# Two exchanges in a hand-written order: P V of unit 13 and the first row of o and wo in the seventh stretch, half of wo and a turn of o in the fifth

## The chip, the cores and the metric

The kernel runs on one core of a Trainium2 chip. The metric is the device time of one execution in microseconds (us), median over runs. Traces and profiles are of one profiled execution each.

## The reference, cut to what matters

The input x has 2048 tokens of width 640. It is layer-normed to xn, and two things are computed from it: attention over the last 512 cached keys with 32 heads of width 192, and a gate from two selected tokens that pass a small feed-forward block. The result is x + s * g.

```
def _A_ref(x, k_cache, v_cache, wq, wo):          # x is xn here
    q = (x @ wq).reshape(B, Sq, Hq, Dh)           # 32 heads of 192
    k = k_cache[:, :, Sk - W:, :]                 # W = 512 keys
    v = v_cache[:, :, Sk - W:, :]
    scores = einsum("bhqd,bhkd->bhqk", q, k) * (Dh ** -0.5)
    p = softmax(scores)
    o = einsum("bhqk,bhkd->bhqd", p, v)
    return o.reshape(B, Sq, Hq * Dh) @ wo         # s

return x + s * silu(_B_ref(xn, ...))
```

## The kernel before, in words

The attention is cut into units. A unit n is a pair of heads and a block of 128 tokens; there are 256. Units come in steps of four (512 tokens of one pair of heads), and steps in the order: groups of four heads, then blocks of 512 tokens, then the two pairs of heads of the group. So units 0 to 3 are the first 512 tokens for the first pair of heads, units 4 to 7 the same tokens for the second pair, units 8 to 15 the next 512 tokens for both pairs, and so on.

For a unit TensorE computes the scores of both heads (`scores`, lines 331 and 338: a part of depth 128 and one of depth 64), VectorE their negated row maximum (`row_max`, line 346), ScalarE the exponentials with their sums (`exps`, line 353), and a DMA transpose on SyncE's queue turns the probabilities from `pexp` into `pT` (`p_turn`, line 358). Then TensorE multiplies them with v (`o_mul`, line 372: 8 matmuls of 192 columns into one PSUM tile `o_ps`; this is "P V" below), VectorE or ScalarE scales the product with the reciprocal sums into `o_sb` (`o_out`, lines 387 and 385), and a second DMA transpose turns `o_sb` into `oT` (`o_turn`, line 393).

The last product joins both pairs of heads of a group: a row w of o and wo (`w_mul`, line 420) takes the turned o of one unit of each pair, three chunks of 128 of each, and multiplies them with the group's wo. It does this for two halves of 320 output columns, six matmuls each, so a row has twelve, into two PSUM tiles `w_ps`; in each half the first three matmuls use the first pair's unit, the last three the second pair's. Row 0 uses units 0 and 4, row 1 units 1 and 5, row 2 units 2 and 6. `w_out` (lines 432 and 434) puts a half into `s_acc`. The weights wo of a group come in two loads of 480 KB (`wo_load`, line 140): `wo.g.0` has the three chunks of the first pair, `wo.g.1` those of the second. So the first three matmuls of a half need the first load and the last three the second.

Units are worked in stretches. The first two hold two units each, every later one three: stretch 4 (counted from 0) has units 10 to 12, stretch 6 has units 16 to 18. While the scores and exponentials of a stretch are worked, the products P V, the projections q and the rows w of earlier stretches are put between them. There is no scheduler: the schedule is manual, and each engine and each DMA queue works in the order in which the program emits its instructions. Of the stretches 0 to 10 this order is written out by hand, token by token, in the string `FIRST`; each begins with `S.j`, the scores of stretch j. From stretch 11 on the functions `stretch` and `end_stretch` write the order by a rule. The tokens that matter here are:

- `S.6`: scores of units 16 to 18; `M.n.h`, `E.n.h`: row maximum and exponentials of unit n, head h; `P.n`: turn of the probabilities
- `O.n` and `Oe.n.e`: P V of unit n and its scaling (e: `v` VectorE, `a` ScalarE); with `O.n.g` its PSUM tile comes from the pool `ps_p` and not from `ps_f`
- `T.j` and `T.j.lo.hi`: turn of o of stretch j, or of its units lo to hi alone. `T.2.0.1` turns unit 4, `T.2.1.3` units 5 and 6
- `W.w` and `We.w.e`: row w of o and wo, and its way into `s_acc`
- `wo.g.h`: the load of a half of wo

All DMAs named here, loads and transposes, are issued from SyncE, in program order. The PSUM pool `ps_p` has six buffers. Scores, the halves of a row and the `.g` tokens take their tiles from it, so the six score tiles of a stretch fill it, and later tiles get a buffer when its reader (an exp, a scaling, a copy) is done. The pool `ps_f` has two buffers, for the q projections and the other products P V.

Of the kernel before, what the change touches and what calls it, by code (L numbers as in the profile page):

```python
# [21 lines left out]
def kernel(ctx, tc, A_x, A_k_cache, A_v_cache, A_wq, A_wo, B_x, B_w_r, B_w_gate, B_w_up, B_w_down, out):  # L22
    nc = tc.nc
    P = 128
    _, S, D = A_x.shape
# [3 lines left out]
    W = min(4096, max(256, Sk // 4))  # L29
# [426 lines left out]
    M = {}  # L456
# [413 lines left out]
S.1 q.1.2 ap.5.g M.2.0 ap.7.g E.2.0 M.2.1 q.1.0.2.4 ap.6.g xT.4.6 q.1.0.0.2.g bn.10.0 qe.1.2.a M.3.0 M.3.1 R.0 bn.10.1 xT.6.8 E.2.1 qe.1.0.0.2.a qe.1.0.2.4.a q.1.1 P.2 bn.11.0 O.0 bn.11.1 bn.8.0 E.3.0 E.3.1 qe.1.1.a Oe.0.v P.1 bn.8.1   # L870
S.2 x.3.0.4 v.1 q.2.1.0.2 as.9 M.4.0 M.4.1 q.2.0 M.6.0 E.4.0 pw.8.12 E.4.1 q.2.2.g M.5.0 qe.2.1.0.2.a E.5.0 qe.2.0.v M.6.1 ap.10.g E.6.0 ap.9.g P.3 E.6.1 M.5.1 q.3.1 qe.2.2.v ap.8.v R.1 ap.11.g O.2 qe.3.1.v Oe.2.v E.5.1 
S.3 M.8.0 M.7.0 P.4 P.5 M.8.1 q.2.1.2.4 M.7.1 R.2 xT.8.10 M.9.0 as.13 bn.15.0 M.9.1 E.8.0 E.7.0 E.8.1 q.3.2 bn.14.0 xT.10.12 E.7.1 P.6 qe.2.1.2.4.a q.3.0.g qe.3.0.a qe.3.2.v E.9.0 E.9.1 O.1.g O.5.g O.4.g Oe.4.a Oe.1.v P.8 as.12 Oe.5.v O.3 
S.4 P.7 bn.15.1 M.10.0 q.4.1 M.11.0 M.12.0 M.11.1 Oe.3.a q.4.0 P.9 M.10.1 qe.4.1.v E.10.0 M.12.1 E.11.0 T.0 E.11.1 q.5.0.g E.10.1 wo.0.0 wo.0.1 T.2.0.1 E.12.0 E.12.1 R.3 qe.4.0.a O.8.g O.7 P.10 Oe.7.a qe.5.0.v T.1 Oe.8.v R.4 bn.14.1 pw.12.16 
S.5 ap.12.g O.6 M.13.0 P.11 E.13.0 M.15.1 Oe.6.a M.15.0 E.15.0 E.15.1 q.4.2 M.13.1 P.12 q.5.2.g M.14.1 M.14.0 qe.4.2.v O.9 E.13.1 Oe.9.a qe.5.2.v E.14.0 W.0 We.0.v E.14.1 
S.6 M.17.0 P.13 M.17.1 ap.14.g M.16.1 O.10 M.18.1 Oe.10.a M.16.0 ap.13.g E.17.0 q.5.1 E.17.1 qe.5.1.v T.2.1.3 E.16.0 R.5 O.12 O.11.g Oe.11.a M.18.0 E.18.0 Oe.12.a E.16.1 W.1 O.13.g We.1.v E.18.1 ap.15.g xT.13.16 xT.12.13 W.2 We.2.v P.15 Oe.13.a 
S.7 q.6.1 M.19.1 M.19.0 E.19.0 M.20.0 q.6.0 qe.6.0.v P.14 T.4 M.21.0 M.20.1 M.21.1 E.19.1 T.3 q.6.2.g k.2.1.a qe.6.1.a O.14 O.15.g R.6 E.20.0 q.7.1.g E.20.1 Oe.14.a P.17 qe.6.2.a E.21.0 Oe.15.v q.7.0 P.16 E.21.1 P.19 W.3 P.18 W.4 qe.7.1.v R.7 qe.7.0.v We.3.v O.19 We.4.a wq.2.a 
S.8 wq.3.a O.16 Oe.19.v M.22.0 v.2.a M.23.1 E.22.0 Oe.16.v k.3.0.a M.23.0 P.20 E.23.0 wo.1.0.a E.23.1 k.3.1.a T.5 M.22.1 M.24.0 P.21 q.7.2 E.24.0 O.17 Oe.17.v E.22.1 P.22 k.2.0.a W.5 qe.7.2.v M.24.1 We.5.a O.20 P.23 W.6 O.21 We.6.a E.24.1 Oe.20.a Oe.21.a O.18.g Oe.18.v P.24 
S.9 M.25.0 M.27.1 M.25.1 M.27.0 q.8.1 E.25.0 E.25.1 q.9.0 T.6 M.26.0 qe.8.1.v W.7 E.27.0 E.27.1 E.26.0 M.26.1 R.8 We.7.v P.25 qe.9.0.v E.26.1 q.8.0 T.7 
# [47 lines left out]
```

## Time and profile before

| | us |
|---|---|
| median of 3 runs | 790.81 |
| lowest and highest of them | 790.41, 791.25 |
| the profiled execution | 789.15 |
| its span | 787.4 |

The mean granted TensorE clock of the profiled execution is 0.999 of full speed. The span runs from the first to the last instruction of the trace; the execution's own time is 1.75 us longer. In the rows of the profile each line has a start or a sum in us, an engine, a line of the kernel, an operation, the tiles (out<-in), their sizes and a count. PE is TensorE's matmuls, PEld its weight loads, DVE VectorE, ACT ScalarE, POOL GpSimd, SPq the queue of SyncE, whose rows show how long an issue took, not the transfer. In the rows of DMA issues the last number is the time from issue to landing. A row that merges several instructions has their count behind it, and its length runs from the first start to the last end; as matmuls are pipelined, the time of a group is better taken from its start to the start of the next group.

### The profile page before, as it was taken

To read this page: it belongs to the slowest core of one execution; us is meant where nothing else is said; L and a number is where in the kernel's file an instruction comes from. 1 tells how busy PE (TensorE), PEld (TensorE's weight loads), DVE (VectorE), ACT (ScalarE), POOL (GpSimd) and SP (SyncE) were. 2 spreads that over 40 slices of the span, in tenths; PEclk is the share of its full clock that TensorE was granted. 3 is DMA by queue.
4 is the path that set the end of the run, shared out by engine and by line. 5 is a ranking of instruction groups with operands and counts; after the bars stand their busy time and mean duration, and the time that the engine had idled before them with its cause. 6 is when DMAs were issued, how large, how long until landed. Compare 5 with 4: busy or idle time off the path is not lost.

```text
span 787.4 us, 15694 instructions
## 1 busy us (share of the span) xinstructions
PE 781.8 (99%) x5767; PEld 482.8 (61%) x5767; DVE 621.7 (79%) x1238; ACT 479.4 (61%) x1299; POOL 179.5 (23%) x198
## 2 busy tenths in 40 slices
PE   8999999999999999999999999999999999999998
PEld 4566656666666666566666655666566666556666
DVE  7976678988888777777777777777788988777786
ACT  8975766565556655565665556565667865565652
POOL 3230000000010000000000699960000000165966
PEclk9999999999999999999999999999999999999999
DMA  9999998899889999999998899779997799997996
GB/s 262 214 202 229 204 199 132 164 175 202 166 147 219 184 195 217 142 221 198 191 222 144 181 180 188 158 141 174 202 172 138 143 193 184 183 194 152 177 167 148
DMA packets 453133, 143.80 MB, mean 183 GB/s; under 512 B 421358, under 2 KB 452720, under 8 KB 453056
## 3 DMA queue, kind: packets, MB, share of 16 engines
q1 hardware_dynamic: 447696, 138.04, 94.0%
q10 hardware_dynamic: 4672, 3.08, 1.4%
q0 software_dynamic: 688, 1.68, 0.9%
q8 instruction: 45, 0.74, 0.4%
q14 instruction: 32, 0.26, 0.1%
HBM read 39.98 MB, written 2.62 MB: 54 GB/s over the span
## 4 chain that ended last, share of the span: by engine, by line
PE 95%; DMA 2%; DVE 1%; ACT 1%; issue 0%; SPq 0%; POOL 0%; DVEq 0%
PE q_ps L317 26%; PE w_ps L420 26%; PE o_ps L372 21%; PE sc L331 14%; PE sc L338 8%; DMA oT<-o_sb 1%; DMA x_in<-in_A_x_dram 1%; ACT pexp L353 1%; DVE nm L346 0%; DVE stats L172 0%; POOL fin_o L447 0%; PE gu_ps L590 0%; ACT o_sb L385 0%; PE y_ps L627 0%; DVE fin_t L445 0%
## 5 line engine op out<-in xcount | busy, mean ns | idle before, releaser
L353 ACT ACTIVATE pexp<-sc,nm 128x512 bf16<-128x512 f32 x512 | 348.5, 697 | 264.1 <-issue 231.7
L346 DVE TENSOR_REDUCE nm<-sc 128x1 f32<-128x512 f32 x512 | 314.9, 682 | 70.9 <-PE sc L338 70.7
L317 PE MATMUL q_ps<-xnT,wq_p 128*128 128x512 bf16 (+1 forms) x985 | 225.4, 374 | 0.5 <-DMA wq_p<-in_A_wq_dram 0.5
L420 PE MATMUL w_ps<-wo_g,oT 128*128 128x320 bf16 (+1 forms) x1542 | 223.0, 298 | 0.1
L420 PEld LDWEIGHTS <-oT 128*128 128x128 bf16 x1542 | 150.4, 98 | 69.5 <-DMA oT<-o_sb 0.4
L372 PE MATMUL o_ps<-v_sb,pT 128*128 128x192 bf16 x2048 | 184.8, 246 | 0.0
L372 PEld LDWEIGHTS <-pT 128*128 128x128 bf16 x2048 | 171.4, 98 | 14.0 <-issue 2.8
L317 PEld LDWEIGHTS <-wq_p 128*128 128x128 bf16 x985 | 89.7, 98 | 122.8 <-issue 33.3
L387 DVE TENSOR_TENSOR o_sb<-o_ps,lsum 128x384 bf16<-128x384 f32 x240 | 132.0, 556 | 41.3 <-PE o_ps L372 22.7
L331 PE MATMUL sc<-kT,qT 128*128 128x512 bf16 x512 | 125.5, 379 | 0.1
L434 DVE TENSOR_TENSOR s_acc<-s_acc,w_ps 128x320 f32<-128x320 f32 x192 | 92.5, 483 | 30.7 <-PE w_ps L420 30.7
L353 ACT ACTIVATION_READ_ACCUMULATOR pexp<-sc,nm 128x1 f32 x512 | 110.2, 215 | 0.0
L309 ACT ACTIVATE qT<-q_ps 128x512 bf16<-128x512 f32 (+1 forms) x180 | 98.7, 604 | 0.0
L331 PEld LDWEIGHTS <-qT 128*128 128x128 bf16 x512 | 48.5, 98 | 42.0 <-issue 1.5
L338 PE MATMUL sc<-kT,qT 64*128 64x512 bf16 x512 | 70.2, 380 | 0.0
L338 PEld LDWEIGHTS <-qT 64*128 64x128 bf16 x512 | 18.0, 94 | 46.7 <-issue 35.8
L664 POOL TENSOR_TENSOR s_acc<-s_acc,xn 128x640 f32<-128x640 f32 x16 | 22.9, 1434 | 103.0 <-DVE s_acc L434 102.9
L643 POOL TENSOR_TENSOR xn<-xn,yh 128x640 bf16<-128x640 bf16 x32 | 44.6, 1394 | 2.7
L633 POOL DMA_DIRECT2D y_d<-y_sb x4 | 2.2, 544 | 181.2 <-DVE y_sb L630 181.2
L510 POOL DMA_DIRECT2D c_d<-cand x1 | 0.7, 725 | 162.8 <-DVE cand L508 162.8
L665 POOL TENSOR_TENSOR s_acc<-s_acc,x_fin 128x640 f32<-128x640 f32 x16 | 22.4, 1400 | 61.4 <-DVE s_acc L434 54.3
L642 POOL TENSOR_SCALAR yh<-y_bc,oh 128x640 bf16<-128x640 bf16 x32 | 25.6, 800 | 5.2 <-DMA y_bc<-y_d 3.6
(110 smaller groups left out, 234.1 us busy)
## 6 DMA issues: line engine op xcount, KB each, us to landing
wo_g<-in_A_wo_dram SPq DMA_DIRECT2D x15, 480.0 KB, 4.3
wq_p<-in_A_wq_dram SPq DMA_DIRECT2D x14, 480.0 KB, 4.6
v_sb<-in_A_v_cache_dram SPq DMA_DIRECT2D x15, 384.0 KB, 4.3
k_raw<-in_A_k_cache_dram SPq DMA_DIRECT2D x28, 192.0 KB, 3.2
pT<-pexp SPq DMA_TRANSPOSE x256, 3.6
x_fin<-in_A_x_dram SPq DMA_DIRECT2D x16, 160.0 KB, 2.7
wgu<-in_B_w_gate_dram SPq DMA_DIRECT2D x15, 128.0 KB, 3.3
wgu<-in_B_w_up_dram SPq DMA_DIRECT2D x15, 128.0 KB, 3.6
```

Of the source, the lines that this page charges most:

```text
L309: nc.scalar.activation(out=out, in_=in_, func=ACT.Copy, scale=scale)
L317: nc.tensor.matmul(q_ps, lhsT=wq_of[g * PAIRS + pr][:, dc, c * P:(c + 1) * P], rhs=xnT[:, t5 * 4 + lo:t5 * 4 + hi, dc, :], start=(dc == 0) ...
L331: nc.tensor.matmul(sc_of[n][hh], lhsT=qT_of[i][:, 2 * hh, u * P:(u + 1) * P], rhs=kp[:, :, 2 * hh, :], start=True, stop=False)
L338: nc.tensor.matmul(sc_of[n][hh], lhsT=qT_of[i][hs, 1, u * P:(u + 1) * P], rhs=kp[hs, :, 1, :], start=False, stop=True)
L346: nc.vector.tensor_reduce(out=nm_of[j][:, c:c + 1], in_=sc_of[n][hh], axis=AX.X, op=ALU.max, negate=True)
L353: nc.scalar.activation(out=pe_of[n][:, hh, :], in_=sc_of[n][hh], func=ACT.Exp, bias=nm_of[j][:, c:c + 1], scale=1.0, accum_out=l_of[j][:, ...
L372: nc.tensor.matmul(ps[:, hh, :], lhsT=pT_of[n][:, hh, jj, :], rhs=v_sb[:, hh, jj, :], start=(jj == 0), stop=(jj == NJ - 1))
L387: nc.vector.tensor_tensor(out=osb_of[j][:, m], in0=ps, in1=l_of[j][:, 2 * m:2 * m + 2].unsqueeze(2).to_broadcast([P, 2, Dh]), op=ALU.mult)
L420: nc.tensor.matmul(w_ps, lhsT=oT_of[j][:, stretches[j].index(n), c % 3, :], rhs=wo_of[g][:, c, lo:hi], start=(c == 0), stop=(c == CPG - 1))
L434: nc.vector.tensor_tensor(out=acc, in0=acc, in1=w_ps, op=ALU.add)
L642: nc.gpsimd.tensor_scalar(out=yh, in0=M["y_bc"][:, j, :], scalar1=M["oh"][:, n, j:j + 1], scalar2=0.0, op0=ALU.mult, op1=ALU.add)
L643: nc.gpsimd.tensor_tensor(out=xn[:, n, :], in0=xn[:, n, :], in1=yh, op=ALU.add)
```

## The change

Two pairs of tokens in the string `FIRST` change places. In stretch 4 (the fifth) the load of the second half of wo stands behind the turn of unit 4 and no longer ahead of it. In stretch 6 (the seventh) P V of unit 13 stands ahead of row 1 of o and wo and no longer behind it. Nothing else differs. The two lines, cut round the places:

```
-S.4 ... E.11.0 T.0 E.11.1 q.5.0.g E.10.1 wo.0.0 wo.0.1 T.2.0.1 E.12.0 E.12.1 R.3 qe.4.0.a O.8.g O.7 P.10 Oe.7.a ...
+S.4 ... E.11.0 T.0 E.11.1 q.5.0.g E.10.1 wo.0.0 T.2.0.1 wo.0.1 E.12.0 E.12.1 R.3 qe.4.0.a O.8.g O.7 P.10 Oe.7.a ...

-S.6 ... T.2.1.3 E.16.0 R.5 O.12 O.11.g Oe.11.a M.18.0 E.18.0 Oe.12.a E.16.1 W.1 O.13.g We.1.v E.18.1 ap.15.g xT.13.16 xT.12.13 W.2 We.2.v P.15 Oe.13.a
+S.6 ... T.2.1.3 E.16.0 R.5 O.12 O.11.g Oe.11.a M.18.0 E.18.0 Oe.12.a E.16.1 O.13.g W.1 We.1.v E.18.1 ap.15.g xT.13.16 xT.12.13 W.2 We.2.v P.15 Oe.13.a
```

Between the tokens `W.1` and `O.13.g` there is no instruction of another engine, so on the other engines nothing changes its order in stretch 6. In stretch 4 the same holds for SyncE's queue round the exchanged pair.

More of the change, by code (lines that the diff above doesn't have):

```diff
@@ L872 @@
 S.3 M.8.0 M.7.0 P.4 P.5 M.8.1 q.2.1.2.4 M.7.1 R.2 xT.8.10 M.9.0 as.13 bn.15.0 M.9.1 E.8.0 E.7.0 E.8.1 q.3.2 bn.14.0 xT.10.12 E.7.1 P.6 qe.2.1.2.4.a q.3.0.g qe.3.0.a qe.3.2.v E.9.0 E.9.1 O.1.g O.5.g O.4.g Oe.4.a Oe.1.v P.8 as.12 Oe.5.v O.3
-S.4 P.7 bn.15.1 M.10.0 q.4.1 M.11.0 M.12.0 M.11.1 Oe.3.a q.4.0 P.9 M.10.1 qe.4.1.v E.10.0 M.12.1 E.11.0 T.0 E.11.1 q.5.0.g E.10.1 wo.0.0 wo.0.1 T.2.0.1 E.12.0 E.12.1 R.3 qe.4.0.a O.8.g O.7 P.10 Oe.7.a qe.5.0.v T.1 Oe.8.v R.4 bn.14.1 pw.12.16
+S.4 P.7 bn.15.1 M.10.0 q.4.1 M.11.0 M.12.0 M.11.1 Oe.3.a q.4.0 P.9 M.10.1 qe.4.1.v E.10.0 M.12.1 E.11.0 T.0 E.11.1 q.5.0.g E.10.1 wo.0.0 T.2.0.1 wo.0.1 E.12.0 E.12.1 R.3 qe.4.0.a O.8.g O.7 P.10 Oe.7.a qe.5.0.v T.1 Oe.8.v R.4 bn.14.1 pw.12.16
 S.5 ap.12.g O.6 M.13.0 P.11 E.13.0 M.15.1 Oe.6.a M.15.0 E.15.0 E.15.1 q.4.2 M.13.1 P.12 q.5.2.g M.14.1 M.14.0 qe.4.2.v O.9 E.13.1 Oe.9.a qe.5.2.v E.14.0 W.0 We.0.v E.14.1
-S.6 M.17.0 P.13 M.17.1 ap.14.g M.16.1 O.10 M.18.1 Oe.10.a M.16.0 ap.13.g E.17.0 q.5.1 E.17.1 qe.5.1.v T.2.1.3 E.16.0 R.5 O.12 O.11.g Oe.11.a M.18.0 E.18.0 Oe.12.a E.16.1 W.1 O.13.g We.1.v E.18.1 ap.15.g xT.13.16 xT.12.13 W.2 We.2.v P.15 Oe.13.a
+S.6 M.17.0 P.13 M.17.1 ap.14.g M.16.1 O.10 M.18.1 Oe.10.a M.16.0 ap.13.g E.17.0 q.5.1 E.17.1 qe.5.1.v T.2.1.3 E.16.0 R.5 O.12 O.11.g Oe.11.a M.18.0 E.18.0 Oe.12.a E.16.1 O.13.g W.1 We.1.v E.18.1 ap.15.g xT.13.16 xT.12.13 W.2 We.2.v P.15 Oe.13.a
 S.7 q.6.1 M.19.1 M.19.0 E.19.0 M.20.0 q.6.0 qe.6.0.v P.14 T.4 M.21.0 M.20.1 M.21.1 E.19.1 T.3 q.6.2.g k.2.1.a qe.6.1.a O.14 O.15.g R.6 E.20.0 q.7.1.g E.20.1 Oe.14.a P.17 qe.6.2.a E.21.0 Oe.15.v q.7.0 P.16 E.21.1 P.19 W.3 P.18 W.4 qe.7.1.v R.7 qe.7.0.v We.3.v O.19 We.4.a wq.2.a
```

## The prediction

> **What bounds the kernel now.** I read the page first, then the chain of waits between 50 and 58.5 us, then the timelines of TensorE, its weight loads, ScalarE and SyncE's queue round the two places of the change, then the landing times of the DMAs issued there.
>
> ```profile
> span 787.4 us, 15694 instructions
> PE 781.8 (99%) x5767; PEld 482.8 (61%) x5767; DVE 621.7 (79%) x1238; ACT 479.4 (61%) x1299; POOL 179.5 (23%) x198
> PE 95%; DMA 2%; DVE 1%; ACT 1%; issue 0%; SPq 0%; POOL 0%; DVEq 0%
> 58.20:780.00 721.80, 721.80 (x5346) 447.90 (x5344) 569.03 (x1121) 428.68 (x1162) 156.57 (x145) 1.00 0.97 180
> ```
>
> The last row is the view by stretches of time: from 58.2 to 780 us TensorE is busy for all 721.80 us at the full granted clock. So whatever TensorE gains or loses before 58 us arrives at the end, unless a later wait on something other than TensorE takes it back. The question is only what TensorE does between 41 and 58 us, where both edits lie.
>
> ```profile
> 50.08 4.59 DMA oT<-o_sb
> 54.66 0.05 issue
> 54.71 1.40 PE w_ps L420 x9
> 56.11 0.66 PE o_ps L372 x8
> ...
> 52.76 1.48 PE L372 MATMUL o_ps<-v_sb,pT 128*128 128x192 bf16 x16
> 54.08 2.02 PE L420 MATMUL w_ps<-wo_g,oT 128*128 128x320 bf16 x12
> 55.94 0.82 PE L372 MATMUL o_ps<-v_sb,pT 128*128 128x192 bf16 x8
> 56.60 1.79 PE L420 MATMUL w_ps<-wo_g,oT 128*128 128x320 bf16 x12
> 58.23 1.46 PE L331 MATMUL sc<-kT,qT 128*128 128x512 bf16 x6
> ...
> 54.00 0.32 PEld L420 LDWEIGHTS <-oT 128*128 128x128 bf16 x3
> 54.70 1.07 PEld L420 LDWEIGHTS <-oT 128*128 128x128 bf16 x9 [0.39 <-DMA oT<-o_sb]
> ```
>
> The first four rows are the chain of waits. It goes through a DMA: the turn of o of units 5 and 6 (T.2.1.3), issued at 50.08, landed at 54.66, and TensorE went on at 54.71 with the nine matmuls that need it. The next five rows are TensorE in order: P V of units 12 and 11, row 1 (W.1), P V of unit 13, row 2 (W.2), the next scores. A row of twelve matmuls without a stall is W.2: 56.60 to 58.23, 1.63 us, 0.136 us each. W.1 takes from 54.08 to 55.94, 1.86 us. So it stalls for **0.23 us**, after its third matmul: unit 1's three chunks are loaded at 54.00, unit 5's not before 54.70. That is the only cost that the first edit can remove.
>
> **The change part by part: P V of unit 13 ahead of W.1.** It adds and removes no instruction. Unit 13's eight matmuls last 56.60 - 55.94 = 0.66 us, and they now run at 54.08, while the turn lands. They need their probabilities turned (P.13) and a free PSUM buffer.
>
> ```profile
> 48.70 1.28 SPq L358 DMA_TRANSPOSE pT<-pexp  x1
> pT<-pexp SPq DMA_TRANSPOSE x1, 3.3
> ...
> 53.74 0.22 ACT L353 ACTIVATION_READ_ACCUMULATOR pexp<-sc,nm 128x1 f32 x1
> 54.02 0.69 ACT L353 ACTIVATE pexp<-sc,nm 128x512 bf16<-128x512 f32 x1
> 54.60 0.19 ACT L353 ACTIVATION_READ_ACCUMULATOR pexp<-sc,nm 128x1 f32 x1
> 54.70 0.72 ACT L385 ACTIVATE o_sb<-o_ps,lsum 128x192 bf16<-128x192 f32 x2
> 55.91 0.19 ACT L353 ACTIVATION_READ_ACCUMULATOR pexp<-sc,nm 128x1 f32 x1
> ```
>
> P.13 is issued at 48.70 and lands 3.3 us later, at 52.0, well ahead of 54.08. The buffers are the finer point. The scores of units 16 to 18 hold all six buffers of the pool ps_p, and every later tile takes one that has been read out. By ScalarE's program order and the rows above, they come free so: the exp of 17.1 ends at 53.96, of 16.0 at 54.79, the two scalings of unit 11's o at 55.42, the exp of 18.0 at 56.10. The profile does not show which tile takes which buffer; I take them in the order of release. Then W.1's two halves now hold those of 17.1 and 16.0, and P V of 13 that of unit 11. After the change P V of 13 takes that of 17.1 (free at 53.96, so it starts at 54.08 as W.1 did), W.1's first half takes that of 16.0, its second half that of unit 11.
>
> So W.1, which could start at 54.08 + 0.66 = 54.74, waits for 54.79 plus the 0.05 us that the chain shows between a landing and TensorE's start: **54.84**. Its fourth matmul comes at 54.84 + 3 x 0.136 = 55.25, 0.6 us behind the landing of 54.66: the old stall is gone. Its second half starts at 55.66, behind 55.42: no wait. W.2 follows at 54.84 + 1.63 = 56.47 and finds buffers free since 56.10 (exp of 18.0) and about 56.4 (first eviction of W.1, wanted only at 57.3). It started at 56.60, so the gain is 56.60 - 56.47 = **0.13 us**. The bounds: 0.23 us if the first half gets an earlier buffer, and nothing if all of the gain waits elsewhere. I take 0.13, since its two ends are measured rows.
>
> No instruction changes its place on VectorE or ScalarE: the scaling of unit 13's o stays behind the exp of 18.1, over 1 us after its product is done either way. The queues of SyncE and GpSimd are not touched by this edit.
>
> What is late next is the chance of losing the 0.13 us again:
>
> ```profile
> 80.82 1.62 PE L331 MATMUL sc<-kT,qT 128*128 128x512 bf16 x6
> 81.02 0.56 DVE L387 TENSOR_TENSOR o_sb<-o_ps,lsum 128x384 bf16<-128x384 f32 x1 [2.97 <-PE o_ps L372]
> ```
>
> These six scores take 1.62 us against 1.46 at 58.23: a wait of 0.16 us on VectorE's scaling, which itself waits for TensorE's product of o. It moves with TensorE, so it gives nothing back. I found no other such gap up to 780 us, as the full row of 721.80 says.
>
> **The second half of wo behind the turn of unit 4.** Again nothing is added; SyncE's queue changes its order from T.0, wo.0.0, wo.0.1, T.2.0.1 to T.0, wo.0.0, T.2.0.1, wo.0.1.
>
> ```profile
> 40.41 0.57 SPq L140 DMA_DIRECT2D wo_g<-in_A_wo_dram  x1
> 41.03 0.48 SPq L140 DMA_DIRECT2D wo_g<-in_A_wo_dram  x1
> 41.61 1.18 SPq L393 DMA_TRANSPOSE oT<-o_sb  x1
> 42.90 1.33 SPq L358 DMA_TRANSPOSE pT<-pexp  x1
> ...
> wo_g<-in_A_wo_dram SPq DMA_DIRECT2D x1, 480.0 KB, 4.0
> wo_g<-in_A_wo_dram SPq DMA_DIRECT2D x1, 480.0 KB, 4.9
> oT<-o_sb SPq DMA_TRANSPOSE x1, 4.8
> ...
> 46.58 0.82 PE L372 MATMUL o_ps<-v_sb,pT 128*128 128x192 bf16 x8
> 47.24 1.79 PE L420 MATMUL w_ps<-wo_g,oT 128*128 128x320 bf16 x12
> 48.87 1.46 PE L331 MATMUL sc<-kT,qT 128*128 128x512 bf16 x6
> ```
>
> The issues follow each other at once, so the turn moves from 41.61 to 41.03 and the load from 41.03 to about 41.03 + 1.18 + 0.06 = 42.27; P.10 behind them stays at 42.90. Landings now: 44.4, 45.9 and 46.4 (issue plus the latency of its row), so they come in the order of the issues, with 1.5 us for the second half of wo and 0.5 us for the turn. Exchanged, the turn lands at about 44.9 and the load at about 46.4.
>
> Who needs them is row 0 (W.0) at 47.24: it takes 1.63 us to the next scores, the same as W.2, so it stalls for nothing now. The earlier turn therefore frees nobody. The later load is needed by its fourth matmul, at 47.24 + 0.41 = 47.65; at 46.4 it has 1.2 us to spare. By the full latency of 4.9 us from its new issue it would land at 47.2, still in time. I take **nothing** for this edit. Above is the rival below; below nothing is excluded, since TensorE waits for neither DMA here.
>
> The Trainium skill, page "DMA: Bandwidth & Descriptors", section "Rules for kernel authors", speaks against this edit: "Issue the DMA early, do compute, wait on its semaphore late". Here the time from issue to need falls from 47.65 - 41.03 = 6.6 us to 5.4 us; the trace's 4.9 us lies below both, so by the rule the edit is a loss of cover and by the rows not yet a loss of time.
>
> Sum: 787.4 - 0.13 = 787.3 us of span. The profiled execution took 789.15 us, 1.7 below the median of 790.81 that the three runs show (790.41 to 791.25); I carry the difference over: 790.81 - 0.13 = **790.7 us**.
>
> **Rivals.**
>
> *Wo late: slower.* If the second half of wo lands after 47.65, W.0's fourth matmul waits and everything behind it. It decides at a latency of 47.65 - 42.27 = 5.4 us.
>
> ```profile
> DMA to landing us min/median/max: 3.8/4.4/5.3
> wq_p<-in_A_wq_dram ACTq DMA_DIRECT2D x1, 480.0 KB, 6.2
> v_sb<-in_A_v_cache_dram ACTq DMA_DIRECT2D x1, 384.0 KB, 6.4
> ```
>
> Against it: none of the sixteen loads of wo took over 5.3 us (first row). For it: loads queued behind others near 71 us took 6.2 and 6.4. Then it lands at 48.7 and W.0 loses 1.0 us: 790.81 + 1.0 - 0.1 = 791.7 at most, 791.1 to 791.7 in general.
>
> *No stall to remove: a new wait instead of the old one.* T.2.1.3 landed 4.6 us after issue, where its neighbour P.13 took 3.3.
>
> ```profile
> 52.50:54.00 1.50, 1.50 (x17) 1.33 (x16) 1.50 (x4) 1.46 (x5) 0.00 (x0) 1.00 1.30 36
> q8 instruction: 1, 0.02, 2.5%
> ```
>
> From 52.5 to 54 the queues moved 36 GB/s, against 183 over the span, and one packet of instructions was fetched between 51.5 and 54.7. If that is an accident of the profiled execution, the turn usually lands at 50.08 + 3.3 = 53.4, W.1 does not stall now (it needs it at 54.49), and the change only adds the wait of 54.84 - 54.74 = 0.10 us: 790.9. For it: the hole in the traffic. Against it: instruction fetches follow the program, which is the same in every run.
>
> *A larger stall than the profile's.* If the turn commonly lands later still, P V of 13 covers up to its own 0.66 us: 790.81 - 0.66 = 790.15. Against it: 54.66 is already the late case beside its neighbours.
>
> *Full gain.* W.1's first half finds an earlier buffer: -0.23, 790.6.
>
> **How the numbers follow.** Chances: forecast 0.48, full gain 0.10, a new wait 0.20, wo late 0.13, larger stall 0.09. Likeliest is 790.7. The range takes in the spread of the three runs (0.40 below, 0.44 above their median) round the first three cases, which gives 790.2 to 791.35, and reaches to the other two: up to 791.7 for wo late, down to 789.9 for half of the larger stall with the spread. A measurement of this kernel can tell about 0.2%, 1.6 us, from no change: below 789.2 or above 792.4. No case reaches either bound by itself. Only the larger stall with its spread (789.75) and late wo with its spread (792.1) come near, so most of the chance is within: faster 0.04, same 0.90, slower 0.06.
>
> **What would show it.** In the profile after, the order at 54 us is P V, W.1, W.2 without P V between; W.1's twelve matmuls are near 1.63 us apart from start to next start, and no weight load of line 420 waits for the DMA of oT. A start of W.1 at 54.84 with the exp of line 353 just ahead shows the buffer's wait; at 54.74 it is the full gain. W.0 still takes 1.63 us; if it takes longer behind its third matmul, wo is late. The issues read wo_g, oT, wo_g, with wo landing before 47.65. The prediction is wrong if the scores at 58.23 move by other than 0.1 to 0.25 us, or if a TensorE gap appears after 58 us that was not there.

## The result, and the profile after

The changed kernel takes 792.41 us (median of 22 runs, 790.19 to 795.01) against 790.11 us before (22 runs, 789.21 to 791.47). The ratio is **1.0026, with a 95% interval of 1.0018 to 1.0034**: slower, where 0.1 us faster was forecast. The times spread twice as wide as before: ten lie from 790.2 to 792.0 and twelve from 792.3 to 795.0, with no wide gap between them. The twelve are called the upper group below. The profiled execution took 792.93 us and is one of them.

The page of the changed kernel, its span, busy times and shares of the chain of waits:

```profile
span 791.2 us, 15694 instructions
PE 782.4 (99%) x5767; PEld 482.7 (61%) x5767; DVE 621.8 (79%) x1238; ACT 480.1 (61%) x1299; POOL 179.7 (23%) x198
PE 91%; DMA 4%; ACT 2%; DVE 1%; issue 0%; SPq 0%; POOL 0%; ACTq 0%; DVEq 0%
```

The work is the same to 0.6 us of TensorE, but the chain now spends 4% in DMAs where it spent 2%. Which DMAs, the chain between 43 and 84 us tells (start, length, what):

```profile
43.28 0.57 SPq L140
...
43.96 5.92 DMA pT<-pexp
...
49.99 1.46 ACT pexp L353 x4
...
51.49 0.59 PE sc L331 x2
...
72.85 10.37 DMA pT<-pexp
...
83.27 1.49 PE o_ps L372 x16
```

The chain goes first through SyncE's issue of the moved load (43.28) and through the turn queued behind it, P.10, which took 5.92 us. It gates exponentials, and these the scores. The second DMA on the chain is far from both edits: the turn of unit 21 (`P.21`), 10.37 us long. TensorE in order, at the first and at the second place:

```profile
48.11 0.57 PE L420 MATMUL w_ps<-wo_g,oT 128*128 128x320 bf16 x3
48.97 1.38 PE L420 MATMUL w_ps<-wo_g,oT 128*128 128x320 bf16 x9 [0.28 <-DMA wo_g<-in_A_wo_dram]
50.19 1.89 PE L331 MATMUL sc<-kT,qT 128*128 128x512 bf16 x6
...
54.51 2.14 PE L372 MATMUL o_ps<-v_sb,pT 128*128 128x192 bf16 x24
56.60 3.42 PE L420 MATMUL w_ps<-wo_g,oT 128*128 128x320 bf16 x24
...
79.49 1.79 PE L420 MATMUL w_ps<-wo_g,oT 128*128 128x320 bf16 x12
83.27 1.49 PE L372 MATMUL o_ps<-v_sb,pT 128*128 128x192 bf16 x16 [1.99 <-DMA pT<-pexp]
```

W.0 is split behind its third matmul: 0.86 us from 48.11 to 48.97 where three matmuls take 0.41, so it waits **0.45 us** for the second half of wo. The six scores behind it last 1.89 us instead of 1.46: **0.44 us** with the finer marks of single matmuls (0.20 and 0.24). The three products P V and then W.1 and W.2 follow each other with no split: the stall that the first edit aims at, 0.22 us, is gone. At 83.27 TensorE has waited **2.16 us**: W.6 started at 79.49 and takes 1.63. The waits in brackets are shorter, because the ends of matmuls are modelled.

One more difference lies ahead of both edits. The next two fences show the same P V of unit 8 in before and after:

```profile
43.75 0.83 PE L372 MATMUL o_ps<-v_sb,pT 128*128 128x192 bf16 x8
```

```profile
44.62 0.83 PE L372 MATMUL o_ps<-v_sb,pT 128*128 128x192 bf16 x8
```

The "front" of the program is 0.87 us later. That is no effect of the change: up to the exchanged pair the instructions are the same, and T.0, issued ahead of it, is 0.97 us later too (40.06 and 39.09). Over the thirteen further profiled executions below that load wo from SyncE it lies between 43.71 and 45.42, so the execution profiled before had one of the earliest fronts, and its 789.15 us lie 1.0 below the median of before. W.1 now also waits 0.10 us for a PSUM buffer (three P V take 2.09 us to the next start instead of 1.99). The sum: 0.87 + 0.45 + 0.44 + 2.16 + 0.10 - 0.22 = 3.80 us, the whole of the 3.8 us by which the spans differ.

Why the load and everything behind it came late shows SyncE's queue, before and then after (start and length of each issue):

```profile
42.90 1.33 SPq L358 DMA_TRANSPOSE pT<-pexp  x1
44.28 1.58 SPq L393 DMA_TRANSPOSE oT<-o_sb  x1
45.96 4.02 SPq L358 DMA_TRANSPOSE pT<-pexp  x3
```

```profile
43.28 0.57 SPq L140 DMA_DIRECT2D wo_g<-in_A_wo_dram  x1
43.96 1.65 SPq L358 DMA_TRANSPOSE pT<-pexp  x1
45.66 2.43 SPq L393 DMA_TRANSPOSE oT<-o_sb  x1
48.18 4.02 SPq L358 DMA_TRANSPOSE pT<-pexp  x3
```

The load took 5.64 us to land (48.93). The issue of T.1 behind it lasts 2.43 us where it lasted 1.58, and P.11 follows at 48.18: counted from T.0's issue (39.09 before, 40.06 after), 8.12 us behind it and no longer 6.87. SyncE's whole queue runs 1.25 us later from here on; at P.21 (70.26 in before, 72.85 in after) it is 1.6 us, again counted from T.0.

### The profile page after: what moved, and what is told of

It reads as the page before. It is cut to its first block, busy times and chain, and to the rows that moved or that the text cites. A ratio compares the mean times of both kernels' runs of the same rounds, so it can differ in the third digit from the quotient of the medians.

```text
span 791.2 us, 15694 instructions
## 1 busy us (share of the span) xinstructions
PE 782.4 (99%) x5767; PEld 482.7 (61%) x5767; DVE 621.8 (79%) x1238; ACT 480.1 (61%) x1299; POOL 179.7 (23%) x198
## 4 chain that ended last, share of the span: by engine, by line
PE 91%; DMA 4%; ACT 2%; DVE 1%; issue 0%; SPq 0%; POOL 0%; ACTq 0%; DVEq 0%
PE w_ps L420 25%; PE q_ps L317 25%; PE o_ps L372 20%; PE sc L331 13%; PE sc L338 8%; DMA pT<-pexp 3%; ACT pexp L353 1%; DMA x_in<-in_A_x_dram 1%; ACT qT L309 0%; DVE nm L346 0%; DVE stats L172 0%; POOL fin_o L447 0%; PE gu_ps L590 0%; ACT junk_a L242 0%; ACT o_sb L385 0%
```

## The experiments

The two traces suggest two theories, and their letters stand in the expectations; L, V and S are told there. **Q** (queue): the moved load delays SyncE's queue; in its narrow form each change from turns to a load leaves a hole in the queue of about a microsecond. **R** (race): the wait near 83 us comes about because ScalarE's loads of wq, on their own queue, get ahead of SyncE's turn of unit 21. In before that turn was issued first, in after it was last. SyncE's turn (the first of four in its row) and ScalarE's two loads in before, then the second load in after:

```profile
70.26 13.16 SPq L358 DMA_TRANSPOSE pT<-pexp  x4
70.57 1.13 ACTq L112 DMA_DIRECT2D wq_p<-in_A_wq_dram  x2
```

```profile
72.64 0.75 ACTq L112 DMA_DIRECT2D wq_p<-in_A_wq_dram  x1
```

Before, P.21 went at 70.26, 0.31 us ahead of the first load, and landed in 7.0 us. After, it went at 72.85, 0.21 us behind the second load (and 0.66 behind the first, 72.19), and took 10.4. The rival to both is **F**: the front, which differs from one execution to the next, makes the difference.

### Each edit alone: e1_pv_only and e2_wo_only

```
e1: ... E.16.1 W.1 O.13.g We.1.v ...      ->  ... E.16.1 O.13.g W.1 We.1.v ...
e2: ... E.10.1 wo.0.0 wo.0.1 T.2.0.1 ...  ->  ... E.10.1 wo.0.0 T.2.0.1 wo.0.1 ...
```

> Only the exchange in the seventh stretch (P V of unit 13 ahead of W.1); the loads of wo stay as before. Theory Q (the second half of wo behind the turn makes SyncE's queue change from transposes to a load twice, each change leaves a hole of about 1 us, the queue runs 1.2 us later up to 70 us and loses its place ahead of ScalarE's weight loads): nothing of that happens here, so 789.9 to 790.4 us, within 0.2 us of before, W.1 without a stall, no wait of 2 us near 80 us. Theory L (only the later landing of wo costs, 0.45 us at W.0, the 2 us near 80 us being accident or shared by all): also about 790.1. Theory V (moving P V of 13 is what costs, by new buffer waits): 792, and a spread from 790 to 795 as with the whole change.

> Only the exchange in the fifth stretch (second half of wo behind the turn of unit 4). Theory Q: the whole loss, 792 to 793 us in the median, runs between 790 and 795; W.0 stalls about 0.4 us after its third matmul, SyncE's queue about 1.2 us later at P.11 against T.0, and TensorE waits up to 2 us for the turn of the probabilities of unit 21 near 80 us in the slow ones. Theory L: 790.5 to 790.7. Theory V: 790.1.

Measured: e1 789.89 us (788.93 to 793.52, 12 runs), ratio 1.0001 (0.9990 to 1.0012); e2 791.49 us (790.58 to 792.09, 11 runs), ratio 1.0013 (1.0005 to 1.0022), against 790.17 for before. TensorE in e1:

```profile
53.85 2.14 PE L372 MATMUL o_ps<-v_sb,pT 128*128 128x192 bf16 x24
55.94 3.42 PE L420 MATMUL w_ps<-wo_g,oT 128*128 128x320 bf16 x24
59.19 1.46 PE L331 MATMUL sc<-kT,qT 128*128 128x512 bf16 x6
```

The 24 matmuls of W.1 and W.2 run without a split: 3.25 us from start to next start, twice 1.63. The three P V take 2.09 us where 24 x 0.083 is 1.99: the remaining 0.10 us is the wait for the buffer that the prediction derived. And in e2:

```profile
48.91 0.57 PE L420 MATMUL w_ps<-wo_g,oT 128*128 128x320 bf16 x3
49.84 1.38 PE L420 MATMUL w_ps<-wo_g,oT 128*128 128x320 bf16 x9 [0.36 <-DMA wo_g<-in_A_wo_dram]
51.05 1.87 PE L331 MATMUL sc<-kT,qT 128*128 128x512 bf16 x6
...
56.69 0.57 PE L420 MATMUL w_ps<-wo_g,oT 128*128 128x320 bf16 x3
57.66 1.40 PE L420 MATMUL w_ps<-wo_g,oT 128*128 128x320 bf16 x9 [0.41 <-DMA oT<-o_sb]
```

W.0 waits 0.52 us for the load, the scores 0.42, and W.1 waits 0.56 for the turn of o of units 5 and 6, where it waited 0.22: SyncE's queue is late there too. 0.52 + 0.42 + 0.34 = 1.3 us, the difference of the medians. So the loss by the second edit is shown: the load is late, and what is queued behind it is late. No theory had its size: Q had expected 792 to 793 us and L 790.5 to 790.7. V, by which P V costs the loss, falls with e1. There is no wait near 80 us in e2: TensorE and ScalarE lose as much as SyncE, and P.21 (73.27) stays ahead of the first load of wq (73.52).

By the medians the parts do not add up: alone they give nothing that can be told from zero and +1.3 us, together +2.3 (and in a later comparison, below, +1.1). The intervals of the ratios overlap, so the times alone do not show that the edits act on each other; only the traces below speak for it. Nor is a run above 792 us the whole change's alone: e1 has two of twelve (792.08 and 793.52), e2 and e4 one of eleven each, before one of 35. In e1's profile P.21 (71.46) is 0.07 us ahead of the first load (71.53), where it was 0.31 ahead in before, so the first edit by itself brings the race nearer; whether it loses it in those two runs is not shown.

### What holds the queue: e3_turn_first and e4_small_load

```
e3: ... wo.0.0 wo.0.1 T.2.0.1 ...  ->  ... T.2.0.1 wo.0.0 wo.0.1 ...
e4: ... wo.0.0 wo.0.1 T.2.0.1 ...  ->  ... wo.0.0 wo.0.1 T.2.0.1 jl ...
    jl: nc.sync.dma_start(out=<unused tile [128, 64]>, in_=x_v[:, 0, 0:64])
```

> From the kernel before: T.2.0.1 ahead of both loads of wo, so the queue changes from transposes to loads once, as before, and both halves of wo are issued some 1.2 us later than before. Theory Q: no second hole, so SyncE's queue keeps its times from P.10 on, no wait of 2 us near 80 us; W.0 may stall on wo, which lands at about 47.2 against a need at 47.24 (first half) and 47.65 (second half): 0 to 0.6 us, 790.1 to 790.8. Theory L: both loads late, so W.0 stalls at least as long as with the change (0.45 us or more), and the result is at least as bad as the change, 792.

> The kernel before with one more load of 16 KB of x into an unused tile behind T.2.0.1: wo keeps its place and time, but the queue changes from transposes to a load a second time. It adds a load that the reference does not need. Theory Q: the hole alone does the harm: SyncE's queue about 1 us later at P.11 against T.0, 791.5 to 792.5 us with a wide spread, W.0 without a stall. Theory L: wo is in time, so 790.1.

Measured: e3 790.59 us (789.73 to 790.98, 11 runs), ratio 1.0004 (0.9995 to 1.0013); e4 790.45 us (789.96 to 792.42, 11 runs), ratio 1.0002 (0.9994 to 1.0011). In e3 the queue changes from turns to loads once less than in the changed kernel, and P.11 still comes 7.74 us behind T.0 (6.87 before). In e4 it changes once more than before, to a load of 16 KB:

```profile
44.07 0.57 SPq L715 DMA_DIRECT2D junk_l<-in_A_x_dram  x1
44.76 1.24 SPq L358 DMA_TRANSPOSE pT<-pexp  x1
46.04 1.30 SPq L393 DMA_TRANSPOSE oT<-o_sb  x1
47.45 4.02 SPq L358 DMA_TRANSPOSE pT<-pexp  x3
```

No issue behind it gets longer, and P.11 comes at 47.45, 7.12 us behind T.0 (40.33): the small load costs the queue 0.25 us. The narrow form of Q, a hole at each change, falls. What the queue's times go with is the landing of the second half of wo. Behind T.0's issue it lands at 6.8 to 6.9 us in before, e1 and e4, with P.11 at 6.9 to 7.1; at 8.5 in e3 with P.11 at 7.7; at 8.6 to 9.0 in e2, after and e8 with P.11 at 7.9 to 8.2. That the queue waits for the load to drain fits this, but no run takes the size of the load alone apart, so the reason stays an inference. L, for which e3 was to be at least as bad as the change, falls too: in e3's profile W.0 waits for nothing, the scores wait 0.38 us and W.1 0.68. That is 0.8 us more than before; the medians show 0.4, with an interval from -0.4 to +1.0.

### The second place: e8_change_again, e5_loads_later, e6_loads_earlier, e7_pv_loads_later

e8 is the change once more, beside the others. e5 is the change, and e7 the first edit alone, with ScalarE's loads put later; e6 is before with them put earlier.

```
e5, e7: ... O.19 We.4.a wq.2.a / S.8 wq.3.a O.16 Oe.19.v M.22.0 v.2.a M.23.1 E.22.0 Oe.16.v k.3.0.a M.23.0 P.20 E.23.0 wo.1.0.a ...
    ->  ... O.19 We.4.a / S.8 O.16 Oe.19.v M.22.0 M.23.1 E.22.0 wq.2.a wq.3.a Oe.16.v M.23.0 P.20 E.23.0 v.2.a k.3.0.a wo.1.0.a ...
e6: ... We.3.v O.19 We.4.a wq.2.a / S.8 wq.3.a O.16 ...  ->  ... We.3.v O.19 wq.2.a wq.3.a We.4.a / S.8 O.16 ...
```

> The changed kernel itself once more, beside the next three on one chip. Theory R (race: the second half of wo, later, holds SyncE's queue back by 1.2 us, P V of 13 ahead of W.1 brings TensorE and ScalarE forward, and so ScalarE's loads of wq get ahead of the turn of the probabilities of unit 21, which then takes 10 us and makes TensorE wait 2 us): two groups of runs, one near 790.5 and one at 792 to 795, median 791 to 793. Theory S (sum: the change costs what its second part alone costs, 1.3 us, and the rest is scatter between chips): 791.2 to 791.5 in one group.

> The changed kernel with ScalarE's loads wq.2, wq.3 moved behind E.22.0 and v.2, k.3.0 behind E.23.0, some 2 to 3 us later, so that the turn of unit 21 is issued ahead of them. Theory R: the upper group disappears, 790.3 to 790.9 us, no wait of TensorE for pT near 80 us. Theory S: nothing changes, 791.2 or more, as with the change.

> The kernel before, with nothing of the change, but ScalarE's loads wq.2 and wq.3 ahead of its two copies of row 4, some 2.6 us earlier, so ahead of the turn of unit 21 on the DMA engines. Theory R: that alone makes the turn take 10 us and TensorE wait about 2 us: 791.5 to 793 us. Theory S: no effect, 790.1.

> The first part of the change alone (P V of unit 13 ahead of W.1) with ScalarE's loads later as in the run before. Theory R: the first part keeps its 0.2 to 0.3 us and loses the single runs of 791 to 793.5 that it has alone: 789.5 to 790.0 us, spread under 2 us. Theory S: as the first part alone, 789.9 with those runs.

Measured against 790.14 us for before: e8 791.20 (790.02 to 793.71, 11 runs), ratio 1.0018 (1.0008 to 1.0028), three of eleven above 792; e5 791.34 (790.14 to 792.49, 11 runs), 1.0016 (1.0007 to 1.0024), one above 792; e6 795.38 (792.18 to 796.78, 6 runs), 1.0059 (1.0043 to 1.0074); e7 791.43 (789.90 to 791.82, 11 runs), 1.0015 (1.0006 to 1.0024), none above 792.

e6 shows the race with neither edit in the kernel. Its ScalarE queue, the time to landing of its turn of o of stretch 5 (T.5), and TensorE:

```profile
66.96 0.43 ACTq L112 DMA_DIRECT2D wq_p<-in_A_wq_dram  x1
...
67.50 0.54 ACTq L112 DMA_DIRECT2D wq_p<-in_A_wq_dram  x1
```

```profile
oT<-o_sb SPq DMA_TRANSPOSE x1, 11.2
```

```profile
80.92 2.58 PE L420 MATMUL w_ps<-wo_g,oT 128*128 128x320 bf16 x9 [3.96 <-DMA oT<-o_sb]
```

and the view by stretches of time (columns as in the last section) behind that wait:

```profile
82.00:83.00 1.00, 1.00 (x5) 0.56 (x4) 0.00 (x0) 0.36 (x1) 0.00 (x0) 0.50 1.06 350
```

The loads go first. T.5, issued 2.1 us behind the second (69.62), takes 11.2 us instead of 4.6, and TensorE waits 4.1 us for it. So R's mechanism, a turn held back by loads issued ahead of it, is shown, though with a distance of 2.1 us and not of the 0.2 us in after. The loss is larger than the 791.5 to 793 us expected because a second cost follows the wait: the granted TensorE clock falls from 1.00 to 0.50 during it and stays there from 80 to 86 us, and the work from 80.92 to 87.14 takes 2.7 us more than in before. The wait of 2.16 us in after left the clock at 1.00. R's remedy fails: in e5 P.21 lands in 3.8 us, but P.22 now takes 6.0 us (5.0 in before), and a wait comes up at 115 us that before did not have (e8 has one of 0.40 us there too, so that the moved loads make it is not shown):

```profile
114.78 0.83 PE L372 MATMUL o_ps<-v_sb,pT 128*128 128x192 bf16 x8 [0.33 <-DMA pT<-pexp]
```

e7 says the same without the second edit: the moved loads cost 1.2 us by its ratio, 1.5 against e1. The upper group is thinner (one run of 22 in e5 and e7), but the medians are no better than e8's.

### The load on another queue: e9_wo_by_pool and e10_pv_wo_by_pool

If SyncE's queue is held by the load, the load could go by GpSimd. e9 is the change, e10 the first edit alone, with both halves of wo issued there.

```
e9:  ... E.10.1 wo.0.0.g T.2.0.1 wo.0.1.g ...
e10: ... E.10.1 wo.0.0.g wo.0.1.g T.2.0.1 ...
```

> The changed kernel with both halves of wo issued from GpSimd's queue instead of SyncE's, at the same places of the program. Theory R (SyncE's queue is held by the late half of wo, and its delay of 1.2 us lets ScalarE's loads get ahead of the turn of unit 21): SyncE's queue is 0.5 to 1 us earlier than before instead of 1.2 us later, no run above 791.5, median 789.6 to 790.2. Theory S (the late landing of wo at W.0 and plain scatter make the loss): no better than the change, 791 or more.

> The first part of the change alone (P V of unit 13 ahead of W.1), with both halves of wo issued from GpSimd's queue, ahead of the turn of unit 4. Theory R: SyncE's queue is about 1 us earlier, the turn of unit 21 has more lead, the single runs of 791 to 793.5 of the first part alone are gone: 789.3 to 789.9 us. Theory S: as the first part alone, 789.9.

Measured against 790.07 us: e9 793.04 (792.81 to 794.80, 5 runs), ratio 1.0049 (1.0035 to 1.0063); e10 793.90 (792.89 to 795.73, 5 runs), 1.0056 (1.0042 to 1.0070). Both slower by far. GpSimd's issues and TensorE in e9:

```profile
36.62 1.78 POOL L140 DMA_DIRECT2D wo_g<-in_A_wo_dram  x2
```

```profile
42.69 0.83 PE L372 MATMUL o_ps<-v_sb,pT 128*128 128x192 bf16 x8 [1.45 <-DMA pT<-pexp]
...
46.38 0.38 PE L331 MATMUL sc<-kT,qT 128*128 128x512 bf16 x1 [1.78 <-DVE o_sb L387]
```

GpSimd is idle there, so the loads go at 36.6 and no longer at 40.4, get among the turns of SyncE (P.9 takes 6.9 us, T.0 6.0 where it took 2.9), and TensorE waits 1.6 and then 1.95 us. It is the race of e6 at another place: a load on SyncE's queue had a place in the order, and on another queue it has none. W.0 itself waits for nothing now.

### ScalarE held back: e11_act_delay

The change, with two unused copies (`aw`: 128 x 640 on ScalarE) ahead of the first load of wq.

```
... We.4.a wq.2.a  ->  ... We.4.a aw aw wq.2.a
    aw: nc.scalar.copy(out=<unused tile [128, 640]>, in_=xn[:, 0, :])
```

> The changed kernel with two copies of 128x640 on ScalarE, 1.2 us of work whose result nobody uses, ahead of its loads wq.2 and wq.3, at a place where ScalarE is idle in the profile of before: the loads come 1.2 us later, just behind the turn of unit 21. Theory R: the upper group of runs (792 and more) is gone, 790.5 to 791.0 us. Theory S: as the change, 791.2 with runs up to 793.7, or worse by the added work.

Measured: 791.42 us (790.38 to 793.05, 11 runs), ratio 1.0021 (1.0012 to 1.0030), two of eleven above 792. In its profile (790.38 us) the loads start at 72.59, 1.25 us behind P.21, which takes 6.1 us, and TensorE does not wait. R had expected 790.5 to 791.0 us and no run above 792; neither came. But two runs in eleven beside three in eleven of e8 tell nothing apart: as a test of the upper group it is inconclusive.

### What makes the upper group: e12_look_a to e15_look_d

Until here one profile alone had shown the wait of 2.16 us, and it was of the upper group. Four more profiled executions of the changed kernel, with no edit, ask whether that is the rule.

> The changed kernel as it is, one more execution with its trace. Theory R (its times above 792 us are executions in which ScalarE's loads of wq get ahead of the turn of unit 21): a profiled execution above 792 us shows a turn of unit 20, 21 or 22 that takes over 8.5 us, and TensorE waiting over 1.5 us for it between 76 and 86 us; one below 791.5 us shows turns of at most 7.5 us there and no such wait. Rival F (the front of the program, before 43 us, differs from one execution to the next and makes both groups): the executions above 792 us reach the scores behind P V of unit 8 0.8 us or more later than those below, and the waits between 76 and 86 us are alike.

> The same kernel and the same question as the look before: theory R has the difference between executions in the wait for the turns of units 20 to 22 (over 1.5 us above 792 us, below 0.6 us in executions under 791.5 us), rival F has it ahead of 43 us.

> The same kernel and the same question: theory R, a wait over 1.5 us between 76 and 86 us in each execution above 792 us and in none below 791.5 us; rival F, 0.8 us or more ahead of 43 us instead.

> The same kernel and the same question: theory R, a wait over 1.5 us between 76 and 86 us in each execution above 792 us and in none below 791.5 us; rival F, 0.8 us or more ahead of 43 us instead.

They took 792.27, 790.31, 790.14 and 792.59 us. With after and e8 there are six, all times in us. "Front" is the start of P V of unit 8 less that of before (43.75); "lead" is the issue of the second load of wq less that of P.21, so a negative lead has the turn last. P.21 of e12 left no landing in the trace; the issue of P.22 bounds its time.

| execution | time | front | W.0 waits | scores wait | lead | T.5 took | P.21 took | TensorE waits for them | span less before's |
|---|---|---|---|---|---|---|---|---|---|
| e14 | 790.14 | +0.61 | 0 | 0.44 | +0.66 | 4.6 | 6.9 | 0 | 1.0 |
| e13 | 790.31 | +0.98 | 0 | 0.32 | +0.12 | 4.5 | 6.5 | 0 | 1.1 |
| e8 | 790.55 | -0.04 | 0.19 | 0.46 | -0.30 | 7.1 | 7.1 | 0.52 | 1.4 |
| e12 | 792.27 | +1.30 | 0.31 | 0.44 | -0.35 | 7.5 | at most 7.4 | 0.92 | 3.1 |
| e15 | 792.59 | +0.79 | 0.04 | 0.43 | -0.29 | 7.2 | 10.4 | 0.54 + 1.74 | 3.4 |
| after | 792.93 | +0.87 | 0.45 | 0.44 | -0.21 | 6.2 | 10.4 | 2.16 | 3.8 |

In each line front, waits, the 0.22 us gained and the 0.10 us for the buffer add up to the last column within 0.2 us, once the wait at 115 us that e8 (0.40) and e12 (0.27) have is added. Two executions of the table: first e15, with SyncE's issue of T.5, ScalarE's second load, P.21 in the chain of waits, and TensorE.

```profile
70.42 1.91 SPq L393 DMA_TRANSPOSE oT<-o_sb  x1
72.15 0.57 ACTq L112 DMA_DIRECT2D wq_p<-in_A_wq_dram  x1
```

```profile
72.44 10.44 DMA pT<-pexp
```

```profile
82.92 1.25 PE L372 MATMUL o_ps<-v_sb,pT 128*128 128x192 bf16 x13 [1.58 <-DMA pT<-pexp]
```

Then e13, with the same load, SyncE's row of P.21 and the turn behind it, and the time of P.21 to landing.

```profile
72.19 1.39 ACTq L112 DMA_DIRECT2D wq_p<-in_A_wq_dram  x1
```

```profile
72.07 8.52 SPq L358 DMA_TRANSPOSE pT<-pexp  x2
```

```profile
pT<-pexp SPq DMA_TRANSPOSE x1, 6.5
```

In e15 the turn is issued 0.29 us behind the second load and takes 10.4 us; in e13, 0.12 us ahead of it, 6.5. The same holds over the table: a turn late enough to stop TensorE in the four executions with a negative lead, and in neither of the other two. In the profiles of before, e1, e2, e3 and e4 the lead is positive (0.53 to 0.76), and none has a wait there.

The lead tells these executions apart, but it is not shown to be the cause. In e8, e12 and e15 the issue of T.5 itself lasts 1.9 us (e15's row above), where it lasts 1.5 in before, after, e13 and e14, and P.21 is queued behind it: without the 0.4 us more, the three leads would be about +0.1, that of e13. There the collision is already under way when P.21 is issued. T.5 goes 1.2 to 1.3 us ahead of the first load in all three and in e13 alike, so what decides the race between them stays open.

R's number held in two of the three executions above 792 us and failed in the third: e12 waits 0.92 us and not 1.5, for T.5, and most of the rest of its distance is its front (1.30 us), the latest of the six. F alone does not do either: e13 has a later front than after and e15 and is over 2.2 us faster. So in these profiles the upper group is a lost race, or a smaller loss in it with a late front. That every run above 792 us is of this kind cannot be read from runs without a trace.

## Why the prediction was wrong, point by point

- **P V of 13 ahead of W.1: right.** The stall of W.1 goes, the wait for the buffer comes and has the derived size (0.10 us in e1), so the rival of the full gain falls. The net, 0.1 us, is less than a measurement tells: e1's ratio is 1.0001. The rival that there is no stall to remove has nothing for it: each profile with W.1 in its old place has one (0.22 us in before, 0.35 in e6, and 0.56, 0.68 and 0.47 in e2, e3 and e4, whose queue is somewhat later). Whether the stall of before is commonly larger, e1's interval does not tell.
- **The load behind the turn of unit 4 at nothing: this step failed.** It put the load's landing "at about 46.4", with "1.2 us to spare". It took the landings of before and handed them to the other transfer. In before the load landed 6.82 us behind T.0's issue. It was issued 1.28 us later and landed 8.3 to 8.9 us behind T.0 in six executions of the changed kernel, with a latency of 5.1 to 5.6 us instead of 4.9. The transfer did not take over the turn's slot; it moved with its issue and a little more. The second reckoning, the full 4.9 us from the new issue, was nearer and still 0.2 to 0.8 us short. The decision point, 5.4 us, was right: the three executions with 5.41, 5.48 and 5.64 wait at W.0, those with 5.10, 5.27 and 5.35 do not or by 0.04. So the rival "wo late" was the case, but it had its chance from loads that did not follow a turn, and at 0.13 too little. The rule of the Trainium skill that the prediction set against this edit (page "DMA: Bandwidth & Descriptors", section "Rules for kernel authors") has the trace on its side: the cover left was 5.4 us, the load took up to 5.64.
- **"P.10 behind them stays at 42.90": true of the issue and of no use.** Its issue stays (3.81 us behind T.0 before, 3.90 after), but it lands 5.9 us later and not 4.4. What is queued behind the moved load was named as unmoved and not priced: the wait of the scores (0.4 us in each execution) and SyncE's delay (P.11 is 0.7 to 1.3 us later behind T.0 in the six executions and in e2). That makes the loss 1.3 us (e2), where the rival's price had W.0 alone.
- **"a TensorE gap appears after 58 us that was not there": named as what would refute it, not looked for.** The prediction read only TensorE's row of 721.80 us, which is full as long as each turn lands in time. It did not ask how near the later turns come. The rows of 70 us had it: a turn issued 0.31 us ahead of the first load of another queue, and already 7.0 us long. SyncE delayed by about a microsecond, with ScalarE kept forward by the first edit, brings that order to its turning point. This is how the two edits act together: with the second alone TensorE and ScalarE lose their 1.3 us as well, and in the one profile of it the order stays.
- **The range** ended at 791.7 and left out this case altogether. Its lower end of 789.9 does not come out of its terms either (790.81 - 0.33 - 0.40 is 790.1); nothing hangs on that.

None of the kernels beats the one before; e1, the first edit alone, equals it.

## What to carry to other kernels

A transfer that is moved behind another in a queue is to be priced with its whole latency from its new issue, and everything queued behind it with the same delay, to the first consumer of each. A TensorE row without gaps says nothing of how near the next gap is: before an edit delays one queue, look for the places where its transfers are issued just ahead of large loads of another queue, and count the lead. And where an edit brings such an order near its turning point, expect a wider spread of times and not only a shifted median: six profiles with their own times showed what a mean of many runs could not.

## What the runs showed of the hardware that was not expected

The view by stretches of time of the changed kernel (after) round the lost race (from:to, busy times of PE, PEld, DVE, ACT and POOL, granted clock, DMA share, GB/s):

```profile
73.00:73.50 0.50, 0.50 (x4) 0.19 (x2) 0.40 (x1) 0.00 (x0) 0.00 (x0) 1.00 4.35 81
73.50:74.00 0.50, 0.50 (x3) 0.10 (x1) 0.00 (x0) 0.00 (x0) 0.00 (x0) 1.00 0.03 3
74.00:74.50 0.50, 0.50 (x7) 0.21 (x6) 0.04 (x1) 0.00 (x0) 0.00 (x0) 1.00 0.08 9
...
75.00:75.50 0.50, 0.50 (x9) 0.50 (x7) 0.50 (x2) 0.26 (x1) 0.00 (x0) 1.00 1.17 333
```

With turns and loads of both queues issued and not landed, almost no transfer begins for a microsecond (3 and 9 GB/s); half a microsecond later it is 333 GB/s. The view counts a packet, the unit that a DMA engine moves, where it starts. The share of 4.35 in the first row says that the packets which started there took 4.35 times the half microsecond, as a mean of the 16 engines: by these records the engines are not idle in the hole but still at work on packets begun before it. The hole stands where loads begin behind turns, in before too (71 to 72 us, 4 and 10 GB/s, behind a share of 4.69): it is no product of the change, and in after the turn caught in it takes 10.4 us. Why those packets last so long was not tried.

The clock of e6 was not expected either: 1.00 in the stretches before its 4.1 us wait, 0.50 behind it. Just as unexpected was that a few tenths of a microsecond between issues on two queues separate executions whose turn takes 6.5 us from others where it takes 10.4, and that the front of the program moves by up to 1.7 us between executions of the same instructions.
